# Batch 2's keys and values as halves with an accumulating DMA, the weight forms moved, and the last row's tail in three column parts

## The chip, the cores and the metric

One core of one Trainium2 chip. The metric is device time in microseconds (us) of one execution; lower is better. Times of a kernel are medians of its runs. A ratio is the mean time of one kernel's fast runs over that of the other's fast runs of the same rounds, so it is not quite the ratio of the medians quoted beside it. On one core a single run has no known state; where runs carry one, only fast ones are compared. The engines go by their names in the profile: PE is TensorE, which runs the matmuls, DVE VectorE, ACT ScalarE, POOL GpSimd; SP (SyncE) issues DMAs in these kernels. The "software queue" is that of the DMAs issued from POOL.

## The reference

Attention with keys and values pooled over 8 positions, for 8 batches of 8 heads and 576 positions, then a mixture of four experts over all 4608 rows:

```python
k_p = k.reshape(B, H, Sp, 8, D).mean(axis=3)          # v_p likewise; Sp = 72, D = 64
attn = softmax(scale * (q @ k_p.T));  x = attn @ v_p  # x: 4608 rows of 512
for e in range(4):
    h = np.maximum(x @ w1[e], 0.0)                    # 512 -> 1024
    out += p[:, e:e + 1] * (h @ w2[e])                # 1024 -> 512
```

## The kernel before

The rows are worked through in nine chunks of four experts, one "step" for each pair. From the second chunk on, each 2x2 block product is done with seven products in place of eight; for this the kernel makes sums and differences of weight blocks once for each expert ("weight forms", in `w2_t` and in place) and of the hidden layer in each step (on DVE, the last one on POOL). A schedule in "slots" places attention pieces, folds (one half of a batch's pooled rows added to the other) and forms between matmuls; eight slots make a step. Numbered "points" do the same for attention pieces and loads of the first batches.

The parts that the change touches:

```python
def load_half(b, src, nm, half):          # used for batches 3 and up in the kernel before
    raws[(nm, b)] = raw_kv[:, 0 if nm == "kraw" else 1]
    ...                                   # DMA of 4 of the 8 pooled rows
        accum_op=ALU.add if half else ALU.bypass,

def combine_w2(e, engine=nc.vector): ...  # four subtractions of 128x1024, the forms of w2[e]

# loads of the first chunk, all issued from POOL in this order
load_w2(2); load_q_halves(1); load_v(1); load_w2(3); ...
# point 43: load_k(2), whole, into raw_kv
# point 60: load_v(2), whole, into the space of w2_t of experts 2 and 3
[lambda: pool_waits(vps[1]...), lambda: load_v(2)] + combine_w2(1, nc.gpsimd)
# forms of experts 2 and 3 only after batch 2's values are folded, steps 5 to 7
s == 5: nothing[:3] + u[3:] + w2f[:1] + nothing[:2] + w2f[1:2]
s == 6: nothing[:3] + w2f[2:] + nothing[:2] + v3[:1]
s == 7: nothing[:3] + v3[3:] + v3[1:2] + nothing[:2] + v3[2:3]

# the last row block: two halves of 256 columns
for lo in (0, TH):
    last_half(c, e, NR - 1, lo)           # 8 matmuls, one accumulation, 2 stores
```

x of a batch is turned from token rows to feature rows by DMA transposes issued from SP; the hidden layer of the chunk's first step needs all four of them. q and the folded keys are turned the same way.

The softmax here doesn't subtract the row's maximum and nothing guards it: scores larger than these inputs give would overflow.

Of the kernel before, what the change touches and what calls it, by code (L numbers as in the profile page):

```python
# [18 lines left out]
def kernel(  # L19
# [104 lines left out]
            in_=q[0, :, 0:NT, :].rearrange("h (p r) d -> p h r d", r=NR)[:, :, 2 * half:2 * half + 2],  # L124
        )

    def load_q_halves(b):
        raws[("q", b)] = qpool.tile([P, H, NR, D], BF16, name="q_sb")
        for hs in halves:
            nc.gpsimd.dma_start(  # L130
                out=raws[("q", b)][:, hs].rearrange("p h r d -> p h (r d)"),
                in_=q[b, hs, 0:NT, :].rearrange("h (p r) d -> p h (r d)", r=NR),
            )

    def load_q_rem(b):
        if b % 2 == 0:
# [7 lines left out]
    def load_k(b):  # L144
        load_kv(b, k, "kraw")
# [4 lines left out]
    def load_w1(e):  # L150
        rows = moe_w1[e].rearrange("(kc p) f -> p kc f", p=P)
        for fh in range(2):
            for dh in range(2):
# [2 lines left out]
                    in_=rows[:, 2 * dh:2 * dh + 2, fh * FH:(fh + 1) * FH],  # L156
                )

    def load_w2(e):
        rows = moe_w2[e].rearrange("(fc p) d -> p fc d", p=P)  # L160
        for lo in (0, FCH // 2):
            fcs = slice(lo, lo + FCH // 2)
            nc.gpsimd.dma_start(out=w2_bf[:, e, fcs], in_=rows[:, fcs])

    def reload_w2(e):
        rows = moe_w2[e].rearrange("(fc p) d -> p fc d", p=P)
# [50 lines left out]

    def fold_parts(nm, b, hs, last, engine):

        def first():  # L220
            raw = raws[(nm, b)]
            engine.tensor_add(out=raw[:, hs, 0:4, :], in0=raw[:, hs, 0:4, :],
                                 in1=raw[:, hs, 4:8, :])

        def rest():
            raw = raws[(nm, b)]
            engine.tensor_add(out=raw[:, hs, 0:2, :], in0=raw[:, hs, 0:2, :],
                                 in1=raw[:, hs, 2:4, :])
            for out in last(hs):
                engine.tensor_add(out=out, in0=raw[:, hs, 0, :], in1=raw[:, hs, 1, :])  # L230

        return [first, rest] if b == 2 else [rest]

    def key_parts(b):
        engine = nc.vector if b == 2 else nc.gpsimd
# [302 lines left out]
    def second_attention():  # L538

        lo, hi = halves  # L540

        return {
            41: [lambda: fold_keys(1, lo)],
            43: [lambda: fold_keys(1, hi), lambda: load_k(2)],
            47: [second_keys],
            51: [lambda: second_queries(0)],
            52: [lambda: second_queries(1), lambda: load_q(2), lambda: load_q_rem(2)],
            54: [lambda: scores(1, 0)],
            56: [lambda: scores(1, 1), lambda: fold_values(1, lo)],
            58: [lambda: scores(1, 2), lambda: fold_values(1, hi)],  # L550
            60: [lambda: scores(1, 3)],
            61: [lambda: context(1, 0), lambda: turn(1, 0)],
            64: [lambda: context(1, 1), lambda: turn(1, 1)],
            67: [lambda: context(1, 2), lambda: turn(1, 2)],
            69: [lambda: context(1, 3), lambda: turn(1, 3)],
        }

    def attention(c):

        lo, hi = halves  # L560
        b = c + 1
        plan = {}

        def add(n, *what):
            plan.setdefault(n, []).extend(what)

        if c % 2:
            i = c // 2
            q_at = 15 if b < B else 3
            for n, piece in zip((0, 9, 13, 14), (rem_queries, rem_scores, rem_context, rem_turn)):  # L570
                add(q_at + n, lambda piece=piece: piece(i))
        parts = forms_of(b, nc.gpsimd)
        add(25, *parts)
        if b == B:
            return plan
        more, far = b + 1 < B, b + 2 < B
        if c == 1:
            add(4, lambda: queries(b))
            add(6, *key_parts(b)[:2])
            add(7, *key_parts(b)[2:])  # L580
            add(7, lambda: keys(b))
            add(8, lambda: pool_waits(state[("kpT", b)][0:1, 0, 0:1]))
            add(8, lambda: (load_q(b + 1), load_q_rem(b + 1)))
            for pair in range(NPAIR):
                add(8 + 2 * pair, lambda pair=pair: scores(b, pair))
            for n, part in enumerate(value_parts(b)):
                add(9 + n, part)
            mixed = (16, 18, 20, 21)
        else:
            for pair in range(NPAIR):  # L590
                add(2 + 2 * pair, lambda pair=pair: scores(b, pair))
            for n, part in enumerate(value_parts(b)):
                add(4 + n, part)
            mixed = (9, 11, 12, 19)
        for n, r in zip(mixed, range(NR)):
            add(n, lambda r=r: context(b, r))
            add(n + 1, lambda r=r: turn(b, r))
        if more:
            add(8 if c == 1 else 4, lambda: load_half(b + 1, k, "kraw", 0))
            add(11, lambda: queries(b + 1))  # L600
            add(12 if c == 1 else 8, lambda: load_half(b + 1, k, "kraw", 1))
            add(16, *key_parts(b + 1))
            add(21, lambda: load_half(b + 1, v, "vraw", 0))
            add(27, lambda: load_half(b + 1, v, "vraw", 1))
            add(24, lambda: keys(b + 1))
        if far:
            add(28, lambda: (load_q(b + 2), load_q_rem(b + 2)))
        return plan
# [164 lines left out]
    def add(acc, prob, ps):  # L773
        nc.vector.scalar_tensor_tensor(  # L774
            out=acc, in0=ps, scalar=prob, in1=acc, op0=ALU.mult, op1=ALU.add,
        )
# [92 lines left out]
    def down(c, e, j, n):  # L869

        if (c, e) == (B, E - 1) and j and n:
            if n == 1:
                for lo in (0, TH):
                    last_half(c, e, NR - 1, lo)
            return
        first = (0, 3, 7, 12, 16) if (c, e) != (B, E - 1) or j == 0 else (0, FCH)
        early = c == 0 and e in (1, 2) and j == 0
        for at in range(first[n], first[n + 1]):
            r, fc = 2 * j + at // FCH, at % FCH
            if early:  # L880
                r, fc = at // 4 % 2, 4 * (at // 8) + at % 4
            if fc == 0:
                sums[r] = psum_o.tile([P, DM], F32, name="o_ps")
            nc.tensor.matmul(  # L884
                sums[r][:], lhsT=hidden[(c, e)][:, fc, r * P:(r + 1) * P], rhs=w2_bf[:, e, fc, :],
                start=(fc == 0), stop=(fc == FCH - 1),
            )
            if fc == FCH - 1:
                if held is not None and r == NR - 1:
                    held.append(lambda: merge(c, e, r, sums[r]))  # L890
                else:
                    merge(c, e, r, sums[r])

    def last_half(c, e, r, lo):

        o_ps = psum_o.tile([P, DM], F32, tag="o_ps", name="o_ps")
        cols = slice(lo, lo + TH)
        for fc in range(FCH):
            nc.tensor.matmul(  # L899
                o_ps[:, 0:TH], lhsT=hidden[(c, e)][:, fc, r * P:(r + 1) * P],  # L900
                rhs=w2_bf[:, e, fc, cols], start=(fc == 0), stop=(fc == FCH - 1),
            )
        dst = accs[(c, r)][:, cols]
        add(dst, p_all[:, c * NR + r, e:e + 1], o_ps[:, 0:TH])
        store_rem(r, dst, cols)

    def merge(c, e, r, o_ps):
# [30 lines left out]
    with tc.manual_schedule(engines={ENG.PE, ENG.DVE, ENG.Activation, ENG.Pool, ENG.SP}):  # L938
# [26 lines left out]
        load_w2(1)  # L965
        load_k(1)
        load_w1(3)
        load_w2(2)
        load_q_halves(1)
        load_v(1)  # L970
        load_w2(3)
        load_q_rem(0)
# [18 lines left out]
        for s in range(len(steps) + 1):  # L991
# [16 lines left out]
            nothing = [lambda: None] * 4  # L1008
            if s == 3:
                placed.setdefault(60, []).extend(  # L1010
                    [lambda: pool_waits(vps[1][0:1, H - 1, 0:1]), lambda: load_v(2)]
                    + combine_w2(1, nc.gpsimd))
            if s == 1:
                w, u, x = combine_w2(0), combine_w1(0), forms_of(0)
                forms_due.extend([lambda w=w, u=u, n=n: (w[n](), u[n]()) for n in range(3)])
# [3 lines left out]
            elif s == 2:  # L1019
                x[3]()  # L1020
                u1, v1 = combine_w1(1), combine_w1(3)
                forms_due.extend([lambda: (u1[0](), u1[1]()), lambda: (u1[2](), u1[3]())]
                                 + nothing + v1[:2])
            elif s == 3:
                forms_due.extend([v1[3], v1[2]])
            elif s == 4:
                x = forms_of(1)
                forms_due.extend(nothing + nothing[:2] + [
                    lambda: x[0](), lambda: (x[1](), x[2]()),
                ])  # L1030
            elif s == 5:
                x[3]()
                w2f = combine_w2(2)
                forms_due.extend(nothing[:3] + u[3:] + w2f[:1] + nothing[:2] + w2f[1:2])
            elif s == 6:
                v3 = combine_w2(3)
                forms_due.extend(nothing[:3] + w2f[2:] + nothing[:2] + v3[:1])
            elif s == 7:
                forms_due.extend(nothing[:3] + v3[3:] + v3[1:2] + nothing[:2] + v3[2:3])
            elif s == E * B + 1:  # L1040
                reload_w2(E - 1)
            for j in range(2):
# [61 lines left out]
```

## Time and profile before

| | before |
|---|---|
| median time | 503.62 us when the prediction was made, later 503.2 to 503.9 us |
| span of the profiled execution | 501.7 us |
| PE busy | 490.9 us (98%) |
| first matmul of chunk 1's hidden layer | 78.65 us |
| from there to the last matmul's start | 418.67 us |
| from the last matmul's start to the end | 4.36 us |

PE is the bound, busy for 98% of the span, so a difference in time must appear as a break in PE's chain, or at its end. The place that will matter looks like this in the chain of waits of the kernel before (start, length, what):

```profile
74.44 4.26 PE o_ps L884 x19
78.70 5.51 PE h_ps L686 x25
```

The last matmuls of chunk 0 go straight over into the hidden layer of chunk 1. x's last transpose was issued at 75.79 and landed at 78.52: PE had it with a break of 0.11 us.

### The profile page before, as it was taken

Reading aid. Unit: us, or ns where it says so; the run is one execution under the profiler, and the core shown is the slowest. Engines: PE = TensorE matmul, PEld = TensorE weight load, DVE = VectorE, ACT = ScalarE, POOL = GpSimd, SP = SyncE. Lnnn points to the kernel's source line nnn. Section 1 sums busy time; section 2 is a strip of 40 time slices with the busy share of each in tenths; the row PEclk is TensorE's granted clock in tenths of the full one; section 3 lists DMA queues with packets and bytes.
Section 4 is the critical chain, followed back from the end, with each engine's and each line's share of the span. In section 5 each row is a group of like instructions: output and inputs, shape, how many; then the busy total and the mean of one; then the engine's idle time right before and its main releaser. Section 6 shows DMA issues by size and latency. Waiting matters only on the chain.

```text
span 501.7 us, 11093 instructions
## 1 busy us (share of the span) xinstructions
PE 490.9 (98%) x4537; PEld 397.5 (79%) x4547; DVE 362.1 (72%) x651; ACT 290.0 (58%) x541; POOL 196.0 (39%) x177
## 2 busy tenths in 40 slices
PE   8999999999999999999999999999999999999996
PEld 3746554797788888888788888887888888888884
DVE  1367886899987767777777777777777767776674
ACT  3654444765666567665766576666655565556650
POOL 8473360458323562267126722661115111512110
PEclk9999999999999999999999999999999999999999
DMA  9999999684925373836573287433210110012003
GB/s 118 206 205 205 202 182 169 77 105 49 140 57 93 47 76 105 109 48 61 110 119 49 23 136 89 65 40 63 65 22 1 54 43 12 1 43 64 2 1 84
DMA packets 84770, 41.90 MB, mean 84 GB/s; under 512 B 48736, under 2 KB 80224, under 8 KB 84720
## 3 DMA queue, kind: packets, MB, share of 16 engines
q0 software_dynamic: 43216, 22.91, 36.2%
q1 hardware_dynamic: 41104, 17.77, 17.1%
q8 instruction: 35, 0.57, 0.5%
q10 hardware_dynamic: 400, 0.52, 0.3%
q14 instruction: 15, 0.12, 0.1%
HBM read 45.69 MB, written 9.44 MB: 110 GB/s over the span
## 4 chain that ended last, share of the span: by engine, by line
PE 82%; DMA 9%; DVE 4%; POOL 2%; issue 1%; ACT 1%; POOLq 0%; ACTq 0%
PE u_ps L790 37%; PE g_ps L668 37%; DMA w_bf<-in_moe_w_dram 5%; DMA q_sb<-in_q_dram 3%; PE o_ps L884 3%; PE two L280 2%; PE two L403 1%; PE h_ps L686 1%; DMA H_sb<-in_v_dram 1%; DVE acc L774 1%; POOL w_bf L154 1%; DVE H_sb L716 1%; DVE w_t L658 0%; DVE w_t L656 0%; PE o_ps L899 0%
## 5 line engine op out<-in xcount | busy, mean ns | idle before, releaser
L668 PEld LDWEIGHTS <-w_bf 128*128 128x128 bf16 x1848 | 178.7, 98 | 26.4 <-issue 1.3
L774 DVE SCALAR_TENSOR_TENSOR acc<-u_ps,p_all,acc 128x512 f32<-128x512 f32 (+1 forms) x216 | 127.6, 592 | 70.2 <-ACT u_ps L827 65.9
L736 POOL TENSOR_TENSOR h_s<-H_sb,h_s 128x1024 bf16<-128x1024 bf16 x31 | 66.0, 2128 | 240.9 <-DVE h_s L735 228.4
L668 PE MATMUL g_ps<-xT,w_bf 128*128 128x256 bf16 x928 | 129.9, 273 | 0.0
L668 PE MATMUL g_ps<-xf,w_bf 128*128 128x256 bf16 x792 | 109.3, 272 | 0.6 <-DVE H_sb L716 0.2
L790 PEld LDWEIGHTS <-H_sb 128*128 128x128 bf16 x992 | 92.5, 98 | 20.1 <-issue 6.0
L712 ACT COPY r<-g_ps 128x512 f32<-128x512 f32 x136 | 79.7, 586 | 41.4 <-PE g_ps L668 34.3
L790 PE MATMUL u_ps<-w_bf,H_sb 128*128 128x256 bf16 x744 | 102.0, 273 | 0.0
L716 DVE CUSTOM_DVE_ANT_0 H_sb<-g_ps,r 128x512 bf16<-128x512 f32 x136 | 93.5, 687 | 2.8 <-ACT r L712 2.5
L719 ACT ACTIVATE H_sb<-g_ps 128x512 bf16<-128x512 f32 x128 | 76.3, 597 | 18.5 <-PE g_ps L668 18.2
L790 PEld LDWEIGHTS <-h_s 128*128 128x128 bf16 x744 | 72.8, 98 | 8.4
L811 ACT COPY g_ps<-g_ps 128x512 f32<-128x512 f32 x62 | 35.4, 570 | 73.5 <-PE g_ps L668 73.5
L790 PE MATMUL u_ps<-w_t,h_s 128*128 128x256 bf16 x496 | 74.4, 273 | 0.0
L827 ACT COPY u_ps<-u_ps 128x256 f32<-128x256 f32 x62 | 22.2, 358 | 34.1 <-PE u_ps L790 33.7
L790 PE MATMUL u_ps<-w_t,H_sb 128*128 128x256 bf16 x248 | 37.3, 273 | 1.3 <-DVE acc L774 1.3
L790 PE MATMUL u_ps<-w_bf,h_s 128*128 128x256 bf16 x248 | 37.2, 273 | 0.0
L884 PE MATMUL o_ps<-w_bf,H_sb 128*128 128x512 bf16 x145 | 35.6, 379 | 0.5 <-issue 0.2
L284 ACT ACTIVATE expT<-two 72x1024 bf16<-72x1024 f32 x28 | 28.5, 1016 | 0.0
L829 DVE TENSOR_SCALAR acc<-u_ps,p_all 128x512 f32<-128x512 f32 x16 | 12.0, 750 | 19.5 <-ACT u_ps L827 19.5
L884 PEld LDWEIGHTS <-H_sb 128*128 128x128 bf16 x152 | 14.3, 98 | 14.1 <-issue 0.8
L733 DVE TENSOR_TENSOR h_s<-H_sb 128x1024 bf16<-128x1024 bf16 x31 | 21.1, 681 | 2.7 <-ACT H_sb L690 2.7
L394 DVE TENSOR_TENSOR x_tok<-two,inv 128x512 bf16<-128x512 f32 x32 | 22.1, 691 | 1.1
(125 smaller groups left out, 446.9 us busy)
## 6 DMA issues: line engine op xcount, KB each, us to landing
out_dram<-acc SPq DMA_DIRECT2D x32, 256.0 KB, 2.4
w_bf<-in_moe_w_dram POOLq DMA_DIRECT2D x17, 256.0 KB, 8.9
w_bf<-in_moe_w_dram POOLq DMA_DIRECT2D x8, 512.0 KB, 14.5
q_sb<-in_q_dram POOLq DMA_DIRECT2D x6, 512.0 KB, 9.8
raw_kv<-in_k_dram POOLq DMA_DIRECT2D x10, 288.0 KB, 6.7
raw_kv<-in_v_dram POOLq DMA_DIRECT2D x10, 288.0 KB, 6.3
raw_kv<-in_k_dram POOLq DMA_DIRECT2D x2, 576.0 KB, 15.1
w_t<-in_v_dram POOLq DMA_DIRECT2D x2, 576.0 KB, 12.4
```

What stands on the lines that cost most here:

```text
L284: nc.scalar.activation(out=state[("expT", b)][:, 2 * pair:2 * pair + 2].rearrange("j h r s p -> j s (h r) p"), in_=two[0:SP].rearrange("j ...
L394: nc.vector.tensor_tensor(out=x_tok, in0=c_ps[:, :, :, 0:D], in1=inv[:].unsqueeze(3).to_broadcast([P, 2, NPAIR, D]), op=ALU.mult,)
L668: nc.tensor.matmul(bank[:, t, :], lhsT=w1_bf[:, e, block, kc, lo:lo + P], rhs=x[:, kc, :], start=(first and t == 0 and kc == 0), stop=(t = ...
L712: nc.scalar.copy(out=r[:], in_=ps[:])
L716: nc.vector._custom_dve(TENSOR_ADD_SAT, out=out, in0=ps[:], in1=r[:], s0=BIG, s1=0.0)
L719: nc.scalar.activation(out=out, in_=ps[:], func=ACT.Relu)
L736: lambda: nc.gpsimd.tensor_sub(out=s4, in0=a12, in1=s2),
L774: nc.vector.scalar_tensor_tensor(out=acc, in0=ps, scalar=prob, in1=acc, op0=ALU.mult, op1=ALU.add,)
L790: nc.tensor.matmul(out, lhsT=lhs[0][:, lhs[1] + f, lhs[2]], rhs=rhs[0][:, rhs[1] + f, rhs[2]], start=(start and f == 0), stop=(f == FCH // ...
L811: nc.scalar.copy(out=s[:], in_=g[:])
L827: nc.scalar.copy(out=two[:, hi], in_=one[:, lo])
L884: nc.tensor.matmul(sums[r][:], lhsT=hidden[(c, e)][:, fc, r * P:(r + 1) * P], rhs=w2_bf[:, e, fc, :], start=(fc == 0), stop=(fc == FCH - 1),)
```

## The change

Its intent: give batch 2 the half loads that later batches have, which takes four folds off DVE and frees the forms' space earlier; make the forms of expert 2 where DVE is idle; have q of batch 1 sooner; shorten what follows the last matmul.

```diff
-        load_w2(2)
-        load_q_halves(1)
+        for half in range(2):
+            load_w2_half(2, half)
+            load_q_half(1, half)
...
-            43: [lambda: fold_keys(1, hi), lambda: load_k(2)],
+            43: [lambda: fold_keys(1, hi), lambda: load_half(2, k, "kraw", 0)],
...                                            # point 60
-                    [lambda: pool_waits(vps[1]...), lambda: load_v(2)]
-                    + combine_w2(1, nc.gpsimd))
+                    [lambda: pool_waits(vps[1]...), lambda: load_half(2, k, "kraw", 1),
+                     lambda: load_half(2, v, "vraw", 0)] + combine_w2(1, nc.gpsimd)
+                    + [lambda: load_half(2, v, "vraw", 1)])
...                                            # last slot of step 4, after batch 2's keys
-            add(7, lambda: keys(b))
+            add(7, lambda: keys(b), *combine_w2(2))
-                add(9 + n, part)               # value folds, four parts
+                add(10 + n, part)              # two parts
...                                            # forms of expert 3: slots 4, then 3 and 4, then 3
+                forms_due.extend(nothing[:3] + u[3:] + v3[:1])        # step 5
+                forms_due.extend(nothing[:3] + v3[3:] + v3[1:2])      # step 6
+                forms_due.extend(nothing[:3] + v3[2:3])               # step 7
...
-                for lo in (0, TH):
-                    last_half(c, e, NR - 1, lo)
+                for lo, hi in ((0, TH), (TH, TH + P), (TH + P, DM)):
+                    last_part(c, e, NR - 1, lo, hi)
```

The removed `first` of `fold_parts` (the fold from 8 to 4 rows) and the new `load_q_half` and `load_w2_half` are left out here.

More of the change, by code (lines that the diff above doesn't have):

```diff
@@ L125, in load_first_q, with load_q_half @@
         )
-    def load_q_halves(b):
-        raws[("q", b)] = qpool.tile([P, H, NR, D], BF16, name="q_sb")
-        for hs in halves:
-            nc.gpsimd.dma_start(
-                out=raws[("q", b)][:, hs].rearrange("p h r d -> p h (r d)"),
-                in_=q[b, hs, 0:NT, :].rearrange("h (p r) d -> p h (r d)", r=NR),
-            )
+    def load_q_half(b, half):
+        if half == 0:
+            raws[("q", b)] = qpool.tile([P, H, NR, D], BF16, name="q_sb")
+        hs = halves[half]
+        nc.gpsimd.dma_start(
+            out=raws[("q", b)][:, hs].rearrange("p h r d -> p h (r d)"),
+            in_=q[b, hs, 0:NT, :].rearrange("h (p r) d -> p h (r d)", r=NR),
+        )
     def load_q_rem(b):
@@ L157, in load_w1, with load_w2_half @@
                 )
+    def load_w2_half(e, half):
+        rows = moe_w2[e].rearrange("(fc p) d -> p fc d", p=P)
+        fcs = slice(half * FCH // 2, (half + 1) * FCH // 2)
+        nc.gpsimd.dma_start(out=w2_bf[:, e, fcs], in_=rows[:, fcs])
     def load_w2(e):
-        rows = moe_w2[e].rearrange("(fc p) d -> p fc d", p=P)
-        for lo in (0, FCH // 2):
-            fcs = slice(lo, lo + FCH // 2)
-            nc.gpsimd.dma_start(out=w2_bf[:, e, fcs], in_=rows[:, fcs])
+        for half in range(2):
+            load_w2_half(e, half)
     def reload_w2(e):
@@ L218, in fold_parts @@
     def fold_parts(nm, b, hs, last, engine):
-        def first():
-            raw = raws[(nm, b)]
-            engine.tensor_add(out=raw[:, hs, 0:4, :], in0=raw[:, hs, 0:4, :],
-                                 in1=raw[:, hs, 4:8, :])
         def rest():
@@ L230, in rest @@
                 engine.tensor_add(out=out, in0=raw[:, hs, 0, :], in1=raw[:, hs, 1, :])
-        return [first, rest] if b == 2 else [rest]
+        return [rest]
     def key_parts(b):
@@ L578, in attention @@
             add(4, lambda: queries(b))
-            add(6, *key_parts(b)[:2])
-            add(7, *key_parts(b)[2:])
-            add(7, lambda: keys(b))
+            add(6, *key_parts(b)[:1])
+            add(7, *key_parts(b)[1:])
+            add(7, lambda: keys(b), *combine_w2(2))
             add(8, lambda: pool_waits(state[("kpT", b)][0:1, 0, 0:1]))
@@ L892, in down, with last_part @@
                     merge(c, e, r, sums[r])
-    def last_half(c, e, r, lo):
+    def last_part(c, e, r, lo, hi):
         o_ps = psum_o.tile([P, DM], F32, tag="o_ps", name="o_ps")
-        cols = slice(lo, lo + TH)
+        cols, n = slice(lo, hi), hi - lo
         for fc in range(FCH):
             nc.tensor.matmul(
-                o_ps[:, 0:TH], lhsT=hidden[(c, e)][:, fc, r * P:(r + 1) * P],
+                o_ps[:, 0:n], lhsT=hidden[(c, e)][:, fc, r * P:(r + 1) * P],
                 rhs=w2_bf[:, e, fc, cols], start=(fc == 0), stop=(fc == FCH - 1),
@@ L903, in last_half @@
         dst = accs[(c, r)][:, cols]
-        add(dst, p_all[:, c * NR + r, e:e + 1], o_ps[:, 0:TH])
+        add(dst, p_all[:, c * NR + r, e:e + 1], o_ps[:, 0:n])
         store_rem(r, dst, cols)
@@ L967 @@
         load_w1(3)
-        load_w2(2)
-        load_q_halves(1)
+        for half in range(2):
+            load_w2_half(2, half)
+            load_q_half(1, half)
         load_v(1)
@@ L1010 @@
                 placed.setdefault(60, []).extend(
-                    [lambda: pool_waits(vps[1][0:1, H - 1, 0:1]), lambda: load_v(2)]
-                    + combine_w2(1, nc.gpsimd))
+                    [lambda: pool_waits(vps[1][0:1, H - 1, 0:1]), lambda: load_half(2, k, "kraw", 1),
+                     lambda: load_half(2, v, "vraw", 0)] + combine_w2(1, nc.gpsimd)
+                    + [lambda: load_half(2, v, "vraw", 1)])
             if s == 1:
@@ L1032 @@
                 x[3]()
-                w2f = combine_w2(2)
-                forms_due.extend(nothing[:3] + u[3:] + w2f[:1] + nothing[:2] + w2f[1:2])
+                v3 = combine_w2(3)
+                forms_due.extend(nothing[:3] + u[3:] + v3[:1])
             elif s == 6:
-                v3 = combine_w2(3)
-                forms_due.extend(nothing[:3] + w2f[2:] + nothing[:2] + v3[:1])
+                forms_due.extend(nothing[:3] + v3[3:] + v3[1:2])
             elif s == 7:
-                forms_due.extend(nothing[:3] + v3[3:] + v3[1:2] + nothing[:2] + v3[2:3])
+                forms_due.extend(nothing[:3] + v3[2:3])
             elif s == E * B + 1:
```

## The prediction

> **What bounds the kernel now.** I read the page's busy shares first, then the chain of work that ended last for 52 to 140 us, then the DVE and POOL timelines beside it, the tile view of the weight forms, and last the timeline of the final 10 us.
>
> ```profile
> PE 490.9 (98%) x4537; PEld 397.5 (79%) x4547; DVE 362.1 (72%) x651; ACT 290.0 (58%) x541; POOL 196.0 (39%) x177
> PE   8999999999999999999999999999999999999996
> ```
>
> PE is busy in every slice, so only PE's idle places can be won: 501.7 - 490.9 = 10.8 us of span. A fair part of that is the first microseconds and the last 4 us, which the change barely touches. As ends of matmuls are modelled, I also looked at PE start to start (a 256-column matmul normally follows the last after 0.109 us: eight take 0.87 us in the chain). The places that differ near the changed code are these, in the chain:
>
> ```profile
> 41.37 15.59 DMA q_sb<-in_q_dram
> 57.01 0.62 PE qt_ps L338 x8
> 57.63 0.87 PE g_ps L668 x8
> 58.50 0.52 PE qt_ps L338 x8
> ...
> 92.89 0.39 DVE acc L774
> 93.29 0.61 DVE H_sb L716
> 93.94 1.03 PE g_ps L668 x8
> ...
> 116.85 2.15 DVE w_t L656
> 119.00 0.68 DVE acc L774
> 119.72 0.60 PE u_ps L790 x4
> ...
> 130.82 2.15 DVE w_t L658
> 132.97 0.68 DVE acc L774
> 133.69 0.60 PE u_ps L790 x4
> ```
>
> The reader is to see four breaks in an otherwise solid PE chain: (A) PE waits for the first half of the second batch's q, the matmul before started at 55.91 and would normally be followed at 56.13, so 0.88 us; (B) the start at 93.94 comes 0.49 after its predecessor, 0.38 too late, behind a queue of DVE work (two folds of the values at 91.52 and 92.15 stand in the chain just before); (C) 1.09 us between starts at 118.63 plus 0.27 after 120.04, against 0.11 each: 1.14 us lost; (D) 0.77 at 132.92 and 0.27 at 134.02: 0.82 us lost. C and D each have one weight form of 2.15 us on DVE ahead of the accumulation that PE needs. The tile view says that this is not the form's own cost:
>
> ```profile
> L656 DVE TENSOR_TENSOR w_t<-w_bf x2: 678/1455/2232, 95.0 to 116.8; 128x1024 bf16<-128x1024 bf16 x2
> L658 DVE TENSOR_TENSOR w_t<-w_bf,w_t x2: 682/1458/2234, 108.2 to 130.7; 128x1024 bf16<-128x1024 bf16 x2
> ```
>
> Same shape, 0.68 us once and 2.23 us once. The slow ones begin at 116.8 and 130.7, inside POOL subtractions:
>
> ```profile
> 116.34 2.11 POOL L736 TENSOR_TENSOR h_s<-H_sb,h_s 128x1024 bf16<-128x1024 bf16 x1 [1.23 <-DVE h_s L735]
> ...
> 130.31 2.11 POOL L736 TENSOR_TENSOR h_s<-H_sb,h_s 128x1024 bf16<-128x1024 bf16 x1 [3.30 <-DVE h_s L735]
> ```
>
> POOL keeps its 2.11 us; DVE ends some 0.5 us after POOL does.
>
> [...] 0.68 becomes 2.23 us, and POOL, which started first, is not slowed. [...] the second half of a later k stands idle 6.15 us on POOL for the first at 99.66. [...] Here x's transposes, issued at 69.91, landed only at 76.39 while the software queue still ran (the page's slice there moved 182 GB/s); the one issued at 75.79 took 2.7 us.
>
> **The change, part by part.** (1) The order w2(2) low, q low, w2(2) high, q high. 512 KB take 512/205 = 2.5 us at the 205 GB/s that the page's slices show from 13 to 50 us, so q low lands at about 54.4 in place of 56.96, and A's first wait goes. But q high keeps its place: it landed at 58.28, and PE wants it at 56.13 + 0.62 + 0.87 = 57.6. The wait moves to the second half. Gain 0.15 us of the 0.88.
>
> (2) k and v of batch 2 come as two halves, the second added by DMA. That removes four DVE folds of 72x1024 at 0.68 = 2.7 us of DVE work, and the values no longer land in the space of the forms of experts 2 and 3. B's queue holds one of those folds, and the remaining value folds start a place later: I take 0.3 of the 0.38 us.
>
> (3) So the forms of expert 2 can be made in the last slot of step 4, while PE makes the hidden layer from 78.7 to 85.3. DVE finished its work there at 83.67 and stood idle until 86.39. Minus two folds (about 1.3 us), plus four forms at 0.60 start to start (2.4 us), it ends near 84.8, inside the idle time. The forms of expert 3 move to the middle of steps 5 to 7. No form is left in the last slot of those steps, next to POOL's subtraction. C and D go, less the 0.09 us that such a place still shows later (170.03): 1.05 + 0.73 = 1.8 us.
>
> (4) The last row's second 256 columns become 128 + 128. Matmuls with 128 columns follow each other after 0.065 us (eight transposes in 0.52), so 16 take about 1.0 instead of 0.87 us at worst. The last accumulation falls from 0.48 to about 0.35 us (0.75 for 512 and 0.48 for 256 columns: 0.27 per 256). Against that 0.13 us:
>
> ```profile
> 496.67 1.95 SPq L925 DMA_DIRECT2D out_dram<-acc  x3
> 496.67 2.04 ACTq L925 DMA_DIRECT2D out_dram<-acc  x3
> ...
> 497.63 0.48 DVE L774 SCALAR_TENSOR_TENSOR acc<-o_ps,p_all,acc 128x256 f32<-128x256 f32 x1 [0.39 <-PE o_ps L899]
> ```
>
> Of these three issues on each queue the last two, at 497.28 and 498.15, are the halves. One issue takes 0.5 us on SP, 0.6 to 0.8 on ACT. Three on each queue from 497.28 put the last issue at about 498.4, where it was at 498.15. Landing takes 2.2 us after it as before. I put the tail at +0.2 us: the part is meant to shorten the end, and I expect it to lengthen it a little.
>
> Gains: 0.15 + 0.3 + 1.8 = 2.25 us.
>
> **The rivals.** First, the moved loads give the gain back at 70 to 90 us. POOL must now wait for k's first half to land (the whole landed at 71.67; half of 576 KB at 205 GB/s less is about 70.2) before it issues the second half, then values' first half, then makes expert 1's four forms of 2.12 us, which ran from 67.78 to 76.4 and would run from about 71.9 to 80.5. This meets DVE's x forms from 78.64 [...], and it sends the values' second half at about 80.5, into the transposes of q (77.77 to 83.5) and of the keys (83.70 to 86.41, wanted by the scores at 87.57). Where a keys' transpose met a values' load, at 115.67, it took 5.0 us in place of 2.7. For it: hardly 1 us of slack. Against it: DVE saves 1.3 us before the keys. I charge 0.7 us for DVE and the keys and 0.3 for later x transposes; fully it would cost 2 to 2.5 us and leave the time at 503.5 to 504.
>
> Second, the second half of k arrives so late that it blocks DVE in order at 79. It queues behind q of batch 2, which landed at 75.11; later accumulating halves took 6.5 us alone and 9.4 us beside transposes. I expect landing at 76 to 78, just in time. If it came at 83, the time would be about 505.
>
> Third, no rival: C and D go wholly, B too, and step 4 has room: 503.6 - 2.6 = 501.0 or a little under.
>
> A new bound by another engine is unlikely: DVE, the next after PE and its loads, loses work.
>
> **Time and chances.** 503.62 - 2.25 + 0.2 + 1.0 = 502.6 if all charges are paid; they are the least certain terms, and the order of this code looks tuned to fit, so I halve the 1.0: 502.1 us. The range runs from the third rival (501.0, less some run-to-run spread) to the first: 500.5 to 503.9. The runs of before spread over 1.9 us, which is as much as the effect. 2% is 10 us, and all PE idle time is 10.8 us: faster by over 2% has 0.01, slower by over 2%, for which a wait of 10 us would have to appear, 0.01; within 2%, 0.98.
>
> **What would show it right or wrong.** In the changed profile: no DVE weight form over 0.7 us after 90 us, and PE unbroken near 118 and 132 (step 3). The transposes of q at 57 to 58.5 show whether the wait moved to the second half (step 1). The issue of the second k half on POOL, its idle time and landing, and the starts of the hidden layer (78.7) and of the first scores after it (87.57), relative to before, show the first and second rivals. The last issue on ACT, and span end minus last accumulation (501.7 - 498.1 = 3.6 us now), show the tail. I am wrong if C and D stay though the forms have moved[...], or if a wait over 2 us appears between 70 and 90 us.

## The result, and the profile after

The changed kernel took 506.81 us (four runs, 506.23 to 508.35) against 503.75 us: ratio 1.0068, 95% interval 1.0039 to 1.0098. It is slower by some 3 us, outside the range that I gave. The two profiled executions, cut at the same places:

| stretch | before | after | difference |
|---|---|---|---|
| start to the last merge of chunk 0 (on DVE) | 77.02 | 75.66 | -1.36 |
| from there to the hidden layer's first matmul | 1.63 | 6.39 | +4.76 |
| from there to the last matmul's start | 418.67 | 418.26 | -0.41 |
| from there to the end | 4.36 | 4.58 | +0.22 |
| span | 501.7 | 504.9 | +3.2 |

One break makes the loss. The chain of the changed kernel at that place:

```profile
75.66 0.76 DVE acc L913
76.43 0.28 SPq L930
...
76.76 5.14 DMA xT<-x_tok
...
82.05 2.05 PE h_ps L685 x6
```

PE's work on chunk 0 ends at 77.2, and its next matmul waits for x's last transpose, which lands at 81.91. Stretch by stretch (busy time of each engine with its count of instructions, the granted clock of TensorE, the share of DMA, GB/s), first of the kernel before:

```profile
core 0: us, PE busy (x) PEld busy (x) DVE busy (x) ACT busy (x) POOL busy (x), PEclk, DMA share, GB/s
72.00:77.00 5.00, 4.87 (x35) 2.20 (x35) 3.46 (x7) 0.00 (x0) 4.33 (x3) 1.00 1.37 174
77.00:82.00 5.00, 5.00 (x24) 2.18 (x23) 4.01 (x9) 1.75 (x3) 0.00 (x0) 1.00 1.28 207
82.00:86.00 4.00, 3.95 (x22) 1.96 (x21) 1.60 (x5) 2.67 (x6) 0.00 (x0) 1.00 0.66 188
```

and of the changed one, the same columns:

```profile
72.00:77.00 5.00, 4.94 (x31) 2.23 (x29) 3.42 (x6) 0.00 (x0) 4.84 (x4) 1.00 1.24 97
77.00:82.00 5.00, 0.35 (x2) 0.00 (x0) 0.00 (x0) 0.00 (x0) 4.94 (x3) 1.00 1.29 208
82.00:86.00 4.00, 3.96 (x11) 1.48 (x12) 3.87 (x11) 1.19 (x2) 0.24 (x1) 0.60 1.21 203
```

The reader is to see three things. From 77 to 82 PE has two matmuls. From 82 to 86 it has 11 in place of 22, at a granted clock of 0.60: matmuls of 512 columns start 427 ns apart in place of 216. The clock records show half clock for 3.413 us from 82.77. That costs 3.413 / 2 = 1.7 us more; I had left this cost out of every rival. And from 72 to 77 the DMA engines were as busy as before (share 1.24 against 1.37) but moved 97 GB/s in place of 174.

POOL's timeline in the changed kernel says what was moving:

```profile
65.33 0.18 POOL L251 COPY mark<-vp 1x1 bf16<-1x1 bf16 x1 [5.75 <-DVE vp L256]
69.89 1.42 POOL L95 DMA_DIRECT2D raw_kv<-in_k_dram  x1 [4.37 <-DMA raw_kv<-in_k_dram]
70.77 1.39 POOL L95 DMA_DIRECT2D raw_kv<-in_v_dram  x1
71.62 2.70 POOL L655 TENSOR_TENSOR w_t<-w_bf 128x1024 bf16<-128x1024 bf16 x1
...
80.85 1.39 POOL L95 DMA_DIRECT2D raw_kv<-in_v_dram  x1
```

The keys' accumulating half waited 4.37 us for the first half and was issued at 69.89, and the values' first half right behind it. They landed at 78.07 and 80.56. In the kernel before the last such load had landed at 76.55. x's transposes, issued from 68.56, ran beside them. The second one took from 71.11 to 80.48, and the third's issue on SP took 2.77 us in place of 1.2, which held back the fourth. The tile views give the least, median and longest time of the four from issue to landing, before and after:

```profile
DMA to landing us min/median/max: 2.7/4.1/6.5
...
DMA to landing us min/median/max: 4.4/6.4/9.4
```

The forms did what was hoped. The tile view of the changed kernel, after 84 us:

```profile
L656 DVE TENSOR_TENSOR w_t<-w_bf,w_t x2: 684/688/693, 86.3 to 113.5; 128x1024 bf16<-128x1024 bf16 x2
L657 DVE TENSOR_TENSOR w_t<-w_bf,w_t x2: 691/1103/1515, 87.0 to 125.8; 128x1024 bf16<-128x1024 bf16 x2
```

One form is still drawn out, to 1.5 us, but PE has no break there. From 86 to 490 us no break of the kinds B, C and D is left.

### The profile page after: what moved, and what is told of

Same layout as the page of the kernel before. It is cut to its first block, busy times and chain, and to the rows that moved or that the text cites.

```text
span 504.9 us, 11113 instructions
## 1 busy us (share of the span) xinstructions
PE 491.0 (97%) x4545; PEld 397.8 (79%) x4555; DVE 356.8 (71%) x648; ACT 289.9 (57%) x541; POOL 198.1 (39%) x179
## 4 chain that ended last, share of the span: by engine, by line
PE 93%; DMA 3%; POOL 1%; DVE 1%; ACT 1%; issue 1%; SPq 0%; POOLq 0%; ACTq 0%
PE g_ps L667 40%; PE u_ps L789 38%; PE o_ps L883 6%; PE h_ps L685 3%; PE two L279 2%; DMA w_bf<-in_moe_w_dram 2%; PE two L402 2%; PE h_ps L698 1%; DMA xT<-x_tok 1%; POOL H_sb L107 1%; POOL q_sb L122 0%; PE o_ps L898 0%; ACT g_ps L810 0%; PE two L465 0%; PE two L487 0%
```

## The experiments

The first theory: the keys' accumulating half, issued late because it waits 4.37 us for the first half, keeps the DMA engines and so holds back x's transposes; PE idles and is then slowed. The rivals: only the lateness and the number of bytes count, whatever the mode; or DMA has no room at all for these loads here; or the forms and the tail cost something themselves.

| run | what | median us | before us | ratio, 95% interval |
|---|---|---|---|---|
| e3_k2_plain | keys' 2nd half overwrites | 503.69 | 503.88 | 1.0004 (0.9989 to 1.0019) |
| e8_no_k2 | no 2nd half of keys | 505.02, one run | 503.88 | - |
| e4_v_early | values' 1st half early | 503.93 | 503.88 | 1.0007 (0.9990 to 1.0024) |
| e5_k_ahead | keys' 1st half earlier | 504.29 | 503.88 | 1.0019 (1.0002 to 1.0035) |
| e6_warm | break filled with matmuls | 506.81 | 503.32 | 1.0061 (1.0031 to 1.0091) |
| e11_spread | all late loads spread | 504.63 | 503.32 | 1.0022 (0.9997 to 1.0046) |
| e2_before_three_tail | before + tail | 503.62 | 503.32 | 1.0003 (0.9976 to 1.0030) |
| e9_before_q_order | before + q order | 504.05 | 503.32 | 1.0005 (0.9970 to 1.0039) |
| e12_before_forms | before, two forms moved | 504.30 | 503.21 | 1.0013 (0.9999 to 1.0027) |
| e14_forms_q_order | e12 + q order | 503.84 | 503.21 | 1.0012 (0.9999 to 1.0026) |
| e7_form_back | after, one form back | 507.05, one run | 503.21 | - |
| e15_after_again | after, unedited | 506.10 | 503.21 | 1.0063 (1.0046 to 1.0080) |
| e16_v_after_keys | loads placed anew | 502.09 | 503.75 | 0.9965 (0.9952 to 0.9978) |
| e17_no_k_ahead | as e16, keys' 1st half in its old place | 502.04 | 503.75 | 0.9981 (0.9957 to 1.0005) |

Below, "break at 77" and "break at 87" are what the start-to-start distance of PE exceeds its usual 0.22 us by, ahead of the hidden layer (waiting for x's transposes) and ahead of batch 2's first scores (waiting for the keys' transpose).

**The mode of the late load.**

```diff
-            accum_op=ALU.add if half else ALU.bypass,
+            accum_op=ALU.add if half and (b, nm) != (2, "kraw") else ALU.bypass,
```

> The changed kernel with one thing other: the second half of batch 2's keys overwrites instead of accumulating (same bytes, same issue, same wait for the first half; wrong result on purpose). Theory 1 (the accumulating mode is what keeps the DMA engines and starves x's transposes): the late transposes land by about 78.5 us, PE's 5.07 us break at 77 shrinks below 1.5 us, and time falls by 4 to 6.5 us, to 500.5 to 502.5. Theory 2 (only the lateness and the bytes of the loads count, whatever their mode): the break stays at 4 us or more and the time within 1.5 us of 506.8.

The result is wrong by construction, though the comparison with the reference did not notice it. The time fell by 3 us to that of the kernel before. The break at 77 was 2.2 us in place of 4.9, no half clock followed (granted clock 1.00 from 79.8 to 84), and another break of 0.6 us stood at 87. The wait and the stretch in this run:

```profile
75.12 4.56 DMA xT<-x_tok
...
72.00:77.00 5.00, 4.94 (x31) 2.25 (x30) 3.77 (x7) 0.00 (x0) 4.84 (x3) 1.00 1.30 135
```

(The first line is of the chain, the second of the stretches.) The DMA packets, software queue and transposes/stores apart, in kB for each 2 us, make it plainer:

```text
          72-74        74-76        76-78        78-80
before    337 +  34     39 + 221      0 + 532      0 + 442
after     129 +  11    149 +  67    130 +  82    184 + 126
e3        224 +   0    292 +  54     50 + 222      0 + 706
```

With the accumulating half the software queue of the changed kernel moves 130 to 150 kB in 2 us while it lasts (in a second trace of it, e15, 137 and then 214), with the plain one of the same bytes 224 to 292, and x's last three transposes land 2.2 us sooner (the last at 79.69 in place of 81.91). So both theories hold in part: without the mode 2.7 us of break and the half clock are gone, and 2.2 us stay for the lateness. These are not shares that add up: e4, below, keeps the mode, without the values' half behind it, and has a break of 0.5 us. Why accumulating packets move so few bytes is not shown here.

**Without that half, and with the values early.**

```diff
# e8: "lambda: load_half(2, k, 'kraw', 1)," removed from point 60
# e4:
-            43: [..., lambda: load_half(2, k, "kraw", 0)],
+            43: [..., lambda: load_half(2, k, "kraw", 0), lambda: load_half(2, v, "vraw", 0)],
     # and removed from point 60
```

> The changed kernel without the second half of batch 2's keys at all (wrong result on purpose); the values' first half is issued then without waiting for the keys, at about 66 us. Both theories: no break at 77 us and about 500.5 us. If a break of over 2 us stays, then neither theory holds and the transposes are late for another reason.

> The changed kernel with the first half of batch 2's values issued with the keys' first half (about 54 us), so that only the keys' accumulating half is issued at 70 us. Right result. Theory 1 (mode): the accumulating half still runs from 72 to 78 beside the transposes, so the break stays at 2.5 to 5 us, 503.5 to 507 us. Theory 2 (bytes): half of the late bytes are gone, the break falls to 2 us or under, 500.5 to 503.

In e8 (wrong by construction too) the break at 77 was gone, as both theories have it, but a break of 2.2 us had come at 87, with 3.413 us of half clock after it: the values' accumulating half, now issued at 76.08, ran beside the transposes of q and of the keys. So my 500.5 us did not come. In e4 the accumulating half had the software queue to itself and moved 139 to 149 kB in 2 us from 72 to 76, as slow as in the changed kernel; yet the break at 77 was 0.5 us, which speaks for the number of bytes against my first theory, and 1.4 us stood at 87:

```profile
82.92 5.71 DMA kpT<-kp
```

The keys' transpose took 5.7 us, with the values' half issued at 79.38 beside it; in the kernel before it took 2.7. Taking away the first break uncovers this second one, which the first had hidden in the changed kernel. It is the first rival of my prediction.

**The keys' first half ahead of expert 3's w2.**

```diff
-        load_w2(3); load_q_rem(0); load_q_rem(1)
-            41: [lambda: fold_keys(1, lo)],
+            41: [lambda: fold_keys(1, lo), lambda: load_half(2, k, "kraw", 0),
+                 lambda: (load_w2(3), load_q_rem(0), load_q_rem(1))],
```

> The changed kernel with the first half of batch 2's keys put ahead of w2 of expert 3 in the load queue, so that it lands near 63 us instead of 69.3, and the accumulating half can be issued near 65.5 instead of 69.9. Right result. Both theories: the accumulating half lands by about 74, the last transpose of x by 79, the break at 77 under 1 us, 500 to 501.5 us. A new wait for expert 3's w2 near 71 us would show as 1 to 2 us more.

The accumulating half landed at 73.35, but the break at 77 was 1.3 us and the one at 87 0.9 us: x's first transposes still landed only at 76.77 behind the values' first half (76.59). A miss for the expected time.

**The clock.**

```diff
                     if j:
+                        warm(22)
                         up_plain(c, e, range(FCH))
```

> The changed kernel with 22 filler matmuls of 512 columns on zeros put in PE's break at 77 us (about 4.7 us, result unchanged). Theory (PE's idle time itself lowers the granted clock afterwards: 0.60 in 82 to 86 us, eight matmuls of 427 ns in place of 216): the matmuls after the break take 216 ns at once, the granted clock stays 1.0, and the time falls by 1.5 to 2 us, to about 504.9. Rival (the clock falls for another reason, or the filler delays what follows): no change or slower, 506.5 to 508.

The break was filled but for 0.4 us, and the matmuls behind it started 216 ns apart from the first on:

```profile
82.00:86.00 4.00, 3.72 (x18) 1.58 (x17) 3.04 (x9) 1.54 (x3) 0.00 (x0) 1.00 1.19 249
```

From the hidden layer's first matmul to the last matmul this trace took 416.54 us, 1.72 less than the changed kernel's 418.26, which is the 1.7 us of half clock. But the hidden layer itself started 0.8 us later, because x's last transpose landed at 82.73, and the median did not move. So the cost of the clock is shown in the trace; that a filler pays is not.

Without the half clock the stretch is 418.67 - 416.54 = 2.13 us shorter than in the kernel before: that is what B, C and D were worth.

**All late loads spread.** The edit is e5's and e4's together, the two-part tail of before, and the values' accumulating half put off:

```diff
             add(8, lambda: pool_waits(state[("kpT", b)][0:1, 0, 0:1]))
+            add(8, lambda: load_half(2, v, "vraw", 1))
-                add(10 + n, part)
+                add(13 + n, part)
```

> The changed kernel with all three late loads spread: keys' first half ahead of expert 3's w2, values' first half with it (about 55 us), only the keys' accumulating half at about 66 us, the values' accumulating half put off until the keys' transpose has landed (about 87 us) with the value folds three places later; and the last row in two parts as in the kernel before. Theory (x's and the keys' transposes share the DMA engines with these loads and that alone costs the time): both breaks, at 77 and at 87 us, under 0.7 us each, time 499.5 to 501.5, so 0.5 to 0.9% faster than the kernel before. Rival (batch 2 needs these transposes later than the loads allow, whatever their order): a break of over 1 us in another place, 502 to 504.

Both breaks went, to 0.2 us and none. New ones came: 0.5 at 101, 1.5 at 107 and 0.9 us at 118, and the time was no better than before. Two lines of POOL's timeline say why:

```profile
104.70 1.40 POOL L95 DMA_DIRECT2D raw_kv<-in_k_dram  x1 [9.90 <-DMA raw_kv<-in_k_dram]
105.57 2.68 POOL L737 TENSOR_TENSOR h_s<-H_sb,h_s 128x1024 bf16<-128x1024 bf16 x1
```

The values' half at 91 pushed back batch 3's keys; POOL stood 9.9 us for them, and the subtraction that PE needs started only behind that issue, at 105.57.

**The tail, and the order of q, each alone on the kernel before.**

```diff
# e2: last_half -> last_part in three parts, as in the change
# e9: load_w2_half / load_q_half interleaved, as in the change
```

> The kernel before with only the last row in three column parts. My prediction's step 4: the tail (end of the last matmul's accumulation to the end of the span) grows; last accumulation to end from 3.6 to about 4.0 us, time +0.1 to +0.5 us. The change's intent: -0.1 to -0.3 us.

> The kernel before with only the order of expert 2's w2 halves and batch 1's q halves interleaved. My prediction's step 1: the wait moves from the first to the second half of q, gain 0.15 us. What the changed kernel's trace suggests instead: q's second half lands near 57.0 and the whole 0.88 us goes; time -0.5 to -1 us.

Neither is to be told from the kernel before by time. The tail can be read in the traces, where it hardly varies: from the last matmul's start to the end 4.36 to 4.38 us in the six traces with two parts (e9's apart), 4.51 to 4.60 in all nine with three. The issues on the two queues after the last row, in the changed kernel:

```profile
499.57 2.41 SPq L924 DMA_DIRECT2D out_dram<-acc  x4
499.58 2.69 ACTq L924 DMA_DIRECT2D out_dram<-acc  x4
```

The last accumulation was down to 0.35 us, and the last issue stood 0.8 us after its end on ACT (500.91 to 501.71), as ACT was still issuing the parts before. So the tail costs 0.2 us. e9's profiled execution fell in the slow state (602 us, clock 0.79), so its trace is not compared; its three fast runs took 503.39 to 504.35. Where q's second half lands varies over the traces of kernels with the new order, from 56.95 us in the changed kernel to 58.91 in e16, and PE's wait for it with it, from none to 1.8 us.

**The forms moved alone.**

```diff
-                forms_due.extend(nothing[:3] + w2f[2:] + nothing[:2] + v3[:1])
+                forms_due.extend(nothing[:3] + w2f[2:] + v3[:1])
-                forms_due.extend(nothing[:3] + v3[3:] + v3[1:2] + nothing[:2] + v3[2:3])
+                forms_due.extend(nothing[:3] + v3[3:] + v3[1:2] + v3[2:3])
# e14: the same and e9's order
```

> The kernel before, loads and tail untouched; only the two weight forms that stood in the last slot of steps 6 and 7 (beside POOL's subtraction) are moved two slots earlier. Theory [...]: no form over 0.7 us after 110 us, PE unbroken where it broke for 1.09 and 0.77 us, time 1.5 to 2 us less, about 501.7, ratio 0.996 to 0.997. Rival (the forms delay DVE in the new slots as much): no change, 503.3.

> As the run before it, with the interleaved order of expert 2's w2 halves and batch 1's q halves added. If the order is worth what my prediction's step 1 says, 0.15 us less than that run, not to be told from it; if it is worth the 0.88 us that the changed kernel's trace seemed to show, about 501.0.

The rival was right: C and D went, and breaks of 1.1 us at 115 and of about 1.2 us in four pieces from 127 to 131 took their place, because the middle of these steps has no spare time on DVE (its timeline shows no idle place from 111.22 to 118.4 us). A form was slow there as well (1.14 us in place of 0.68, 1.06 of it in the chain), with POOL's folds at 112.33 (1.15 us) and 113.55 (1.62 us for two) beside it:

```profile
112.97 1.06 DVE w_t L656
```

The change gains because it takes forms out of these steps into step 4's idle time. The profiled execution of e14 was its slowest (506.72 us). It shows, in a kernel with the loads of before but for the order of q, a break of 2.2 us at 77 and 3.413 us of half clock: its values landed at 78.14 in place of 76.55. So that break can come with plain loads too, when they end late. One of the runs of before had 507.02 us at a mean clock of 0.996, but no trace of it was kept.

**One form put back in the changed kernel, and the changed kernel again.**

```diff
-                forms_due.extend(nothing[:3] + v3[2:3])
+                forms_due.extend(nothing[:3] + nothing + v3[2:3])
```

> The changed kernel with one form of expert 3 put back in the last slot of step 7, beside POOL's subtraction. Theory [...]: that form takes 2.2 us in place of 0.68 and PE breaks there again, 0.7 to 1 us in total. Rival (in the kernel before those forms were slow for another reason, such as the values' landing place): 0.68 us and no break.

> The changed kernel once more, unedited, to see how far its break at 77 us is its own and how far it varies: a break of 4 to 6 us followed by 3 to 5 us at about half clock if it is its own, 506 to 507.5 us. If the break is under 3 us in this trace, the first trace was an extreme and the mean loss has another part.

In e7 the form beside POOL's subtraction took 2.2 us again, and PE broke by 0.66 and 0.16 us there:

```profile
134.07 2.24 DVE L657 TENSOR_TENSOR w_t<-w_bf,w_t 128x1024 bf16<-128x1024 bf16 x1
...
133.64 2.11 POOL L735 TENSOR_TENSOR h_s<-H_sb,h_s 128x1024 bf16<-128x1024 bf16 x1 [3.09 <-DVE h_s L734]
```

(From the timelines of DVE and of POOL.) So the place beside POOL's subtraction makes a form slow, 2.24 us where the other form of that line took 0.69, and not where the values land. e15 had a break of 4.2 us and 3.413 us of half clock: the loss is the change's own.

**The loads placed anew.** As e11, but the values' accumulating half goes to POOL before its subtraction, as soon as the keys' transpose has landed; e17 is the same with the keys' first half left in its old place:

```diff
-            add(8, lambda: pool_waits(state[("kpT", b)][0:1, 0, 0:1]))
+            add(7, lambda: pool_waits(state[("kpT", b)][0:1, 0, 0:1]),
+                lambda: load_half(2, v, "vraw", 1))
-                add(10 + n, part)
+                add(11 + n, part)
```

> As e11_spread, but the values' accumulating half is issued as soon as the keys' transpose has landed (about 85.5 us), ahead of POOL's subtraction, and the value folds come two places earlier. Theory (e11's breaks at 107 and 117 us were POOL waiting in order for the next keys, which that load had pushed back): no break over 0.7 us from 77 to 150 us, time 500.5 to 501.8, 0.3 to 0.6% faster than the kernel before. Rival (DMA and POOL have no room for these loads anywhere in 50 to 110 us): a break of over 1 us again, 503 to 505.

> As e16_v_after_keys, but the keys' first half in its old place (behind expert 3's w2), the values' first half right after it. Theory: e4_v_early's break of 0.5 us at 77 stays, its 1.4 us at 87 goes; time 500.8 to 502.5. Rival: as for e16_v_after_keys.

e16 is faster than the kernel before by 0.35% (0.22 to 0.48%), about 1.7 us, and so faster than the changed one by over 4. Its chain:

```profile
76.31 3.10 DMA xT<-x_tok
...
79.55 7.07 PE h_ps L687 x32
...
88.47 0.34 PE two L279 x4
```

A break of 0.5 us is left at 77, none at 87, and none over 0.3 us from there to the end. From the hidden layer to the last matmul it takes 416.44 us, e17 416.45, e6 416.54: the gain of the moved forms, whole. e17 has the same median; one of its six runs took 506.02 us, so its interval reaches 1.0005.

## Why the prediction was wrong

- *Step 1, the order of q* (0.15 us). In the changed kernel's trace the whole wait was gone and PE came to 77 us 1.36 us ahead. In its second trace (e15) 0.5 us of wait stood at the second half, as foreseen. Over the traces the wait varies from none to 1.8 us, and alone (e9, e14) the order shows no gain. The step is neither refuted nor of weight; the 1.36 us is lost in the break anyway.
- *Steps 2 and 3, folds and forms* (0.3 and 1.8 us). Right: 2.13 us by e6's trace, 2.2 by e16's and e17's. That the place beside POOL's subtraction was the cause stands by e7 (2.24 us there, 0.69 elsewhere). "No weight form over 0.7 us" was not quite met (one of 1.5 us), without a break.
- *Step 4, the tail* (+0.2 us). Right in sum: +0.2 us in nine traces. Its parts were less so: in the changed kernel the span from the first of these issues on ACT to the last was 1.53 us (500.18 to 501.71), where I had 1.1, and the last one landed after 1.95 us, where I had 2.2.
- *The first rival's charge* is the step that failed: "I charge 0.7 us for DVE and the keys and 0.3 for later x transposes", halved after that to 0.5 us. It measured 4.76 us of longer approach, and 1.7 us of half clock that no step had. The path was wrong, not only the size: I had the values' second half run into the transposes of q and of the keys (that wait exists, 1.4 us in e4, but stays hidden here), and the runs show the keys' second and the values' first half running into x's four transposes, the last of which PE waits for (landed at 81.91, before at 78.52). I had even the landing of the accumulating half about right (76 to 78 us foreseen; 78.07 found, 76.03 in e15) and took it for a question of DVE's order, "just in time" for the fold at 79. The transfer behind it, the values' first half, and what both do to x's transposes, I gave 0.3 us. The trace of before held the warning: a transpose issued at 69.91 beside the loads took 6.5 us, and an accumulating half with transposes beside it 9.4. I quoted both and applied them to the load alone. A third I misread: the halves that took 6.5 us "alone" (issued at 146.79, 199.02 and 252.12) each had transposes of x beside them, the first of which took 5.1, 6.4 and 5.0 us, where one with the software queue idle took 2.4 (issued at 163.99). The sign of being wrong that I had named, a wait over 2 us between 70 and 90 us, is what came.
- *Halving the charges* because "the order of this code looks tuned to fit" was not an argument from the profile. Unhalved I would have had 502.6 us, still wrong.
- The chance of 0.98 for within 2% was right; the range was too narrow on the slow side, since a single wait of 5 us on PE's path was not in it.

What stays open: why an accumulating load moves about half the bytes in the same time here; whether the transposes wait in the DMA engines or in SP's issue; why a form on DVE takes three times as long beside POOL's subtraction; and after which breaks the half clock comes.

## What to carry to other kernels

When a load is moved later or split with a wait between its parts, list every other transfer of that stretch, above all those that the bounding engine waits for, and time them as they run beside it, not alone. When PE may idle for some microseconds, look for a halved clock afterwards and add its cost: here 3.413 us of half clock, 1.7 us lost, came after breaks of 4.9 us (the changed kernel), 4.2 us (e15) and 2.2 us (e8, e14), though not after one of 2.2 us in e3. And undo such a break one load at a time: behind the first one stood a second, and behind that a third on POOL, where an issue that waited 9.9 us stood before PE's subtraction, and only the placement that cleared all three showed the gain that the moved work had had from the start.

## What the traces show of the hardware

- Accumulating loads: the software queue moved 129 to 149 kB in 2 us with the accumulating half in it (137 and 214 in e15, 139 to 149 with that half alone in e4), and 224 to 292 kB with a plain one of the same bytes, with transposes under way in all of them.
- Transposes beside loads: one of x landed 2.4 us after its issue (163.99 in the kernel before) with the software queue idle, and up to 9.4 us beside the two half loads.
- The clock: half clock for 3.413 us followed breaks with 2.37 us (e14) and 2.46 us (e8) from one matmul's start to the next, and did not follow one of 2.42 us (e3).
- DVE beside POOL: in e7 a form of 0.69 us took 2.24 beside POOL's subtraction, and POOL, which had started first, kept its 2.11.
